# An add that read its constant from a PSUM bank now reads it from SBUF, in a new instruction order (attention and mixture kernel, one core)

## The chip, the cores and the metric

The kernel runs on one core of a Trainium2 chip. The metric is the device time of one execution in microseconds (us). Five engines work side by side, each through its own queue in order: TensorE (PE in the rows; its weight loads are PEld), VectorE (DVE), ScalarE (ACT), GpSimd (POOL) and SyncE (SP), which here only issues DMAs. They meet through semaphores: an instruction may wait for a count that another engine's instruction raises when it ends. PE writes only into PSUM, which has 8 banks per partition; DVE and ACT read PSUM and SBUF; POOL reads SBUF.

## The reference, cut to what matters

For 8 batches and 8 heads (sequence 576, head dimension 64) attention keeps only scores close to the row's maximum:

```python
scores = scale * np.matmul(q, k.transpose(0, 1, 3, 2))
thresh = np.max(scores, axis=-1, keepdims=True) - tau
scores = np.where(scores >= thresh, scores, -1000000000.0)
attn = np.exp(scores - max); attn = attn / (sum + 1e-09)
x = attn @ v
```

Then a mixture runs per batch on x (576 x 512): `theta = x @ w_theta`, `zr = x * cos(theta)`, `zi = x * sin(theta)`, `u = x + w_tok_r @ zr + w_tok_i @ zi`, and the output is `u + relu(u @ w_ch)`. All of it is float32; most products are done as three passes over a high and a low part of each operand.

## The kernel before, in words

Heads are worked in 32 pairs n, each in 5 units i: units 0 to 3 take 128 queries of both heads of the pair, unit 4 the last 64 queries of both in one tile. Per unit:

- PE writes the scores (L797, 12 matmuls for two heads, 6 for unit 4) into PSUM: two banks per head. From pair 5 on there is one place for it, banks 0 to 3 (unit 4: banks 0 and 1, or 2 and 3); the first five pairs take turns between banks 0 to 3 and 4 to 7.
- DVE evicts each head's scores to SBUF (tile `sc`) and reduces the row minimum of the negated, scaled scores into `nm` on the way (L817: one instruction and a short accumulator read).
- DVE adds the span `cut` to these minima (L827, the **add**). It is 160 small instructions in the kernel: 128 for two heads (128x2), 32 for one tile (128x1).
- ACT takes the result as a bias: L838 masks, L845 takes the exponential and its row sum.
- DVE transposes in blocks of 32 (L857, L859) into `a`.

Per pair PE then multiplies by v (L874, two parts of 72 matmuls, also into banks 0 to 3), ACT copies the result out (L887, L890), and the row sums are inverted (L900, L901) and spread by DMA. Every fourth pair a batch is full and its mixture is fed into the PE queue between the scores of the next batch: L982 (channel products), L1125 (transposes), L1170 (token products); these use banks 2 to 7. POOL and DVE make the low parts (L527), POOL multiplies (L1100, L928). In the first 170 us the weights are split as well (lines 577 to 669).

The constant that L827 adds lies in PSUM, in two columns of bank 0 that no matmul writes:

```python
cuts = psum[:, 0, 508:510]
nc.vector.tensor_scalar(out=cuts, in0=cut.broadcast_to([P, 2]), scalar1=1.0, scalar2=None, op0=ALU.mult)
```

What stands when in each engine's queue is set by a table, not by a rule that runs: `Plan` collects the operations, and `run()` issues them by the numbers in `ORDER`, with the buffer of each tile taken from `PLACES`. Semaphore waits are put in by the framework underneath, from the tiles and banks that instructions touch; `Plan` itself knows nothing of the read of bank 0 by L827 (its argument `over` names `nm` and `small` alone).

Of the kernel before, what the change touches and what calls it, by code (L numbers as in the profile page):

```python
# [14 lines left out]
ALU = mybir.AluOpType  # L15
# [49 lines left out]
        "0101201210002121201201210210212012120101201021021012010201212010211021"  # L65
    ),
    "xl": (
        "002130211031201232130120301230123012301231023012320130123102301230123012310230123"
    ),
    "xh": (  # L70
        "20012031202031202031130123102301210310201302130123120301230213012302130123120301231203012302130123"
    ),
    "rb": (
        "010101011001010110010001101110010101101000111000"
    ),
    "bank": (
        "73733223675445237632450444004430004447000044604004437643567456754736747656475457465657740000002000000300"
        "00007000000757464657322346275746467475546767546600000040000006000000400000036745765476372635746535676447"
        "65456767000000400000050000007000000745675467574754676574764777754567454600000040000007000000600000066765"
        "74657472675764574566774574564747000000400000040000007000000765545767444657436754564557674556754600000040"  # L80
        "00000500000050000006745645764523426557546564764576777645000000600000060000007000024523475673237434235742"
        "63753467324546"
    ),
    "z": (
        "1012010212001200120012001200120012001200120"
    ),
    "q": (
        "02131023102130213021302130213021302130213021302130213210312"
    ),
    "k": (  # L90
        "02310210321032103210321032103210321032103210321032103210321"
# [5 lines left out]
        "01235976841870231576241035179203102516470235891053145264073154210352406174213056802345126015340241320132"  # L97
        "31402301401526304125064782102312034512436012405212031456710358203461025410231426301521042357682051342610"
        "43501425012340531260351741230451620537112056032415768395410326705401451024321560"
    ),  # L100
    "nm": (
        "01232031032301012012031201202130012100213120102123100120201230102310123012010012301021023102130210213101"
        "20312013021311201010213101201231310210012301230301231010"
# [8 lines left out]
        "01234560132460513426150243610254"  # L112
# [8 lines left out]
        "0123012301231023012310230123012301231023013213020123012301231023"  # L121
    ),
    "zl4": (
        "0123102301231023012301320123012301230123012301230123013201230123"
# [8 lines left out]
        "011000010101010110101101010"  # L133
# [281 lines left out]
def tile_attn_moe(  # L415
# [43 lines left out]
    nc.vector.memset(half_pi, 0.5 * math.pi)  # L459
    magic = small[:, 4 : 5]  # L460
    nc.vector.memset(magic, MAGIC)
    cuts = psum[:, 0, 508:510]
    wt_h = const.tile([P, NK, S], F32R, name="wt_h")
    wt_l = const.tile([P, NK, S], F32R, name="wt_l")
    wm_dram = dram.tile([2, NM, P, 2, NM, P], F32, name="wm_dram")
# [881 lines left out]
```

## Time and profile before

| | |
|---|---|
| time, median of 3 runs | 937.41 us (931.9, 937.41, 938.98) |
| profiled execution, its own time | 931.98 us |
| its span, first to last instruction | 930.2 us |
| PE busy | 858.5 us (92%) |
| ACT busy | 692.4 us (74%) |
| DVE busy | 684.3 us (74%) |
| POOL busy | 340.7 us (37%) |

PE is busy nearly all the time, so the question at any place is what PE waits for there. A matmul that has no wait follows the one before at a distance shorter than its own duration, so busy PE is not PE at its peak.

### The profile page before, as it was taken

To read this page: it belongs to the slowest core of one execution; us is meant where nothing else is said; L and a number is where in the kernel's file an instruction comes from. 1 tells how busy PE (TensorE), PEld (TensorE's weight loads), DVE (VectorE), ACT (ScalarE), POOL (GpSimd) and SP (SyncE) were. 2 spreads that over 40 slices of the span, in tenths; PEclk is the share of its full clock that TensorE was granted. 3 is DMA by queue.
4 is the path that set the end of the run, shared out by engine and by line. 5 is a ranking of instruction groups with operands and counts; after the bars stand their busy time and mean duration, and the time that the engine had idled before them with its cause. 6 is when DMAs were issued, how large, how long until landed. Compare 5 with 4: busy or idle time off the path is not lost.

```text
span 930.2 us, 33724 instructions
## 1 busy us (share of the span) xinstructions
PE 858.5 (92%) x14526; PEld 764.7 (82%) x14526; DVE 684.3 (74%) x1545; ACT 692.4 (74%) x1390; POOL 340.7 (37%) x444
## 2 busy tenths in 40 slices
PE   6677899899999999999999999999999999999998
PEld 3554688788987889988888889988799889988898
DVE  7979878976677885778777876787966768777443
ACT  6986798766876689866898659956898569976550
POOL 1248555533432234523432344232344233431211
PEclk9899999999999999999999999999999999999999
DMA  7546542445323451246432333235633354213502
GB/s 275 177 142 213 172 148 93 143 151 189 145 93 106 160 178 68 80 138 216 164 106 93 114 120 138 105 133 166 190 108 101 98 179 167 89 66 136 188 2 74
DMA packets 45286, 126.13 MB, mean 136 GB/s; under 512 B 5456, under 2 KB 14544, under 8 KB 41040
## 3 DMA queue, kind: packets, MB, share of 16 engines
q1 hardware_dynamic: 44992, 123.97, 39.6%
q8 instruction: 114, 1.87, 0.8%
q14 instruction: 36, 0.29, 0.1%
q10 hardware_dynamic: 144, 0.00, 0.0%
HBM read 110.17 MB, written 13.78 MB: 133 GB/s over the span
## 4 chain that ended last, share of the span: by engine, by line
PE 64%; DVE 21%; ACT 6%; issue 5%; POOL 2%; DMA 1%; SPq 0%; DVEq 0%; ACTq 0%; POOLq 0%
PE banks_ps__66 L1170 18%; PE banks_ps__66 L874 15%; PE banks_ps__66 L797 14%; PE banks_ps__66 L982 12%; DVE sc L817 10%; DVE a L857 5%; PE banks_ps__66 L1125 3%; DVE nm L827 1%; ACT sc L838 1%; DMA v<-in_vp_dram 1%; ACT sc L845 1%; POOL xl L527 1%; PE banks_ps__66 L663 1%; DVE xl L527 1%; DVE xh L603 1%
## 5 line engine op out<-in xcount | busy, mean ns | idle before, releaser
L838 ACT ACTIVATE sc<-sc,nm 128x576 f32<-128x576 f32 x288 | 216.7, 771 | 104.5 <-DVE nm L827 104.2
L817 DVE TENSOR_SCALAR_CACHE_REDUCE sc<-banks_ps__66,small 128x576 f32<-128x576 f32 x288 | 224.4, 808 | 41.4 <-PE banks_ps__66 L797 35.4
L845 ACT ACTIVATE sc<-sc,small 128x576 f32<-128x576 f32 x288 | 222.6, 774 | 4.8
L857 DVE STREAM_TRANSPOSE a<-sc 128x576 f32<-128x576 f32 x256 | 188.7, 759 | 31.0 <-PE banks_ps__66 L874 23.7
L797 PE MATMUL banks_ps__66<-k,q 64*128 64x288 f32 (+1 forms) x1638 | 175.7, 324 | 36.3 <-DVE nm L827 22.5
L797 PEld LDWEIGHTS banks_ps__66<-k,q 64*128 64x128 f32 (+1 forms) x1638 | 132.0, 187 | 70.7 <-DVE nm L827 37.0
L874 PE MATMUL banks_ps__66<-a,v 32*64 32x144 f32 x9216 | 168.7, 289 | 15.2 <-issue 6.0
L874 PEld LDWEIGHTS banks_ps__66<-a,v 32*64 32x64 f32 x9216 | 148.9, 132 | 30.5 <-issue 14.5
L982 PE MATMUL banks_ps__66<-xh,wm 128*128 128x288 f32 x1024 | 169.6, 302 | 3.5 <-issue 1.5
L1170 PE MATMUL banks_ps__66<-wt_h,zh 128*128 128x288 f32 x576 | 160.6, 305 | 1.1 <-ACT zh L1131 1.1
L1170 PE MATMUL banks_ps__66<-wt_l,zh 128*128 128x288 f32 x576 | 158.7, 300 | 0.0
L982 PEld LDWEIGHTS banks_ps__66<-xh,wm 128*128 128x128 f32 x1024 | 143.5, 188 | 14.9 <-issue 10.7
L527 POOL TENSOR_TENSOR xl<-xT,xh 128x288 fp32r<-128x288 f32 x78 | 67.1, 881 | 178.3 <-ACT xh L941 82.1
L1100 POOL TENSOR_TENSOR z<-z,xT 128x288 f32<-128x288 f32 x112 | 88.4, 824 | 95.4 <-ACT z L1081 95.4
L1170 PEld LDWEIGHTS banks_ps__66<-wt_h,zh 128*128 128x128 f32 x576 | 107.9, 189 | 5.6 <-issue 3.1
L1170 PEld LDWEIGHTS banks_ps__66<-wt_l,zh 128*128 128x128 f32 x576 | 108.2, 188 | 2.1 <-issue 2.0
L1170 PE MATMUL banks_ps__66<-wt_h,zl 128*128 128x288 f32 x576 | 96.2, 301 | 0.0
L982 PE MATMUL banks_ps__66<-xl,wm 128*128 128x288 f32 x512 | 94.8, 302 | 1.0 <-POOL xl L527 0.3
L1150 DVE TENSOR_TENSOR zl<-banks_ps__66,zh 128x512 fp32r<-128x512 f32 (+1 forms) x96 | 51.5, 547 | 47.7 <-ACT zh L1131 47.6
L1170 PEld LDWEIGHTS banks_ps__66<-wt_h,zl 128*128 128x128 f32 x576 | 81.1, 188 | 2.7 <-issue 2.5
L527 POOL TENSOR_TENSOR q<-rawq,q 128x320 fp32r<-128x320 f32 x54 | 49.1, 917 | 86.8 <-DVE q L732 64.8
L982 PEld LDWEIGHTS banks_ps__66<-xl,wm 128*128 128x128 f32 x512 | 75.4, 188 | 6.0 <-issue 2.9
(81 smaller groups left out, 921.6 us busy)
## 6 DMA issues: line engine op xcount, KB each, us to landing
v<-in_vp_dram SPq DMA_DIRECT2D x32, 1152.0 KB
wm<-wm_dram SPq DMA_DIRECT2D x64, 512.0 KB
rb<-sums_dram SPq DMA_DIRECT2D x64, 144.0 KB
out_dram<-xT SPq DMA_DIRECT2D x31, 288.0 KB
rawq<-in_qT_dram SPq DMA_DIRECT2D x27, 320.0 KB
rawk<-in_kT_dram SPq DMA_DIRECT2D x27, 288.0 KB
z<-in_w_tok_dram SPq DMA_DIRECT2D x9, 576.0 KB
wm_dram<-rb SPq DMA_DIRECT2D x16, 256.0 KB
```

The costliest lines, as they stand in the source:

```text
L527: eng.tensor_tensor(out=out()[:, c0:c1], in0=in0()[:, c0:c1], in1=in1()[:, c0:c1], op=ALU.subtract)
L797: nc.tensor.matmul(ps()[:, 2 * j + h, :HS], q[a]()[r, i * P : (i + 1) * P], k[c]()[r, h * HS : (h + 1) * HS], start=(x == 0), stop=(x == l ...
L817: lambda j=j, sc=sc: nc.vector.tensor_scalar(out=sc().rearrange("p (a b) -> p a b", a=2), in0=ps()[:, 2 * j : 2 * j + 2, :HS], scalar1=gat ...
L838: lambda j=j, sc=sc: nc.scalar.activation(out=sc(), in_=sc(), func=AF.Prelu, bias=nm()[:, 2 + j : 3 + j], scale=-1.0, alpha=STEEP),
L845: lambda j=j, sc=sc, total=total: nc.scalar.activation(out=keys(sc()), in_=keys(sc()), func=AF.Exp, bias=back, accum_out=pr.rows()[:, tota ...
L857: nc.vector.transpose(out=a()[:, :, j, 32 * i : 32 * i + 32], in_=src.rearrange("p (c q) -> p c q", q=32))
L874: nc.tensor.matmul(ps()[64 * h : 64 * h + 64, b, :w], v()[r, c, h, :], a()[r, c, h, :], start=(c == 0), stop=(c == 17))
L982: nc.tensor.matmul(ps[h]()[:, :HS], wm()[:, a, c, :], parts[c][bb]()[:, h * HS : (h + 1) * HS], start=first and n == 0, stop=final and n = ...
L1100: eng.tensor_tensor(out=zi, in0=zi, in1=x[m]()[:, c0:c1], op=ALU.mult)
L1125: nc.tensor.transpose(out=tp()[:, i * P : (i + 1) * P], in_=z()[:, c : c + P], identity=ident)
L1150: lambda zh=zh, zl=zl, tv=tv: nc.vector.tensor_tensor(out=zl(), in0=tv(), in1=zh().bitcast(F32), op=ALU.subtract),
L1170: nc.tensor.matmul(ps()[:, :HS], zz[c][lo]()[:, zz[c][2]], w[:, c, hs], start=(q + n == 0), stop=(q + n == len(work) - 1),)
```

## The change

Two edits. First, the add takes its constant as a per-partition scalar from SBUF (`cut`, a column of `small`), so it is a tensor_scalar and no longer a tensor_tensor; the copy in PSUM and the instruction that wrote it (L545) are gone. Second, the tables `ORDER` and `PLACES` are new throughout: all instructions but the one are the same, in another order on every engine, and in other buffers. Line numbers fall by up to 3 (L817 is L814, L827 is L824, L874 is L871, and so on).

```diff
@@ PLACES (most entries differ)
     "nm": (
-        "01232031032301012012031201202130012100213120102123100120201230102310123010012010301021023102130210213101"
+        "01232012031201210210231013002130012021013120120123101021201230102310231212010012301021023102130210213101"
...
@@ ORDER (134 lines for 135)
-    "202 1 -3 5 -205 206 1 1 -7 14 1 29 -28 29 -28 -7 -210 1 1 209 2 -210 1 242 -12 1 1 -231 6 197 1 42 -1 3 2 -1 "
+    "203 -1 -202 200 5 2 -6 -200 1 213 -9 11 -1 -8 10 -7 8 -10 36 -242 1 242 -241 242 1 -13 -229 6 225 15 -1 -15 18 "
...
@@ tile_attn_moe
-    cuts = psum[:, 0, 508:510]
...
@@ factors()
-        nc.vector.tensor_scalar(out=cuts, in0=cut.broadcast_to([P, 2]), scalar1=1.0, scalar2=None, op0=ALU.mult)
...
@@ unit()
         dve(
             0.15,
-            lambda: nc.vector.tensor_tensor(out=nm()[:, 2 : 2 + w], in0=nm()[:, :w], in1=cuts[:, :w], op=ALU.add),
+            lambda: nc.vector.tensor_scalar(out=nm()[:, 2 : 2 + w], in0=nm()[:, :w], scalar1=cut, scalar2=None, op0=ALU.add),
             t0 + A("add", n), over, ((nm, 2),), small=True,
         )
```

**PE, scores of one unit of a late pair.** Two rows of before, with the semaphores each waits for: the first matmul of the twelve has the one wait on DVE.

```order
L797 MATMUL banks_ps__66<-k,q 128x288 [waits DVE_49]
L797 MATMUL banks_ps__66<-k,q 128x288 x11
L905 MATMUL banks_ps__66<-ident,rows 9x128 [waits DVE_49,Activation_49]
L982 MATMUL banks_ps__66<-xl,wm 128x288 x4
L982 MATMUL banks_ps__66<-xh,wm 128x288 x4
```

And the same place (the 24th L905, now L902) with the change:

```order
L794 MATMUL banks_ps__66<-k,q 128x288 [waits DVE_49] x2
L794 MATMUL banks_ps__66<-k,q 128x288 x10
L902 MATMUL banks_ps__66<-ident,rows 9x128 [waits DVE_49,Activation_49]
L979 MATMUL banks_ps__66<-xh,wm 128x288 x4
L979 MATMUL banks_ps__66<-xl,wm 128x288 x4
```

The one wait has become two, one on each of the first two matmuls (they write the first bank of head 0 and of head 1). In the built program of before, 87 first matmuls of scores and 26 of values wait for a count that an add raises; with the change none does, and the waits of scores on L817 (now L814) rise from 56 to 155. In the other direction 27 adds waited for PE before, and none does now.

**DVE, about 727 us into the span of before.** The add on `nm_11485` belongs to the last unit whose scores are evicted ahead of a multiplication by v.

```order
L817 TENSOR_SCALAR sc_11484,nm_11485<-banks_ps__66,small_76 128x576 [waits DVE_49,PE_49,Activation_49]
L817 TENSOR_SCALAR sc_11498,nm_11485<-banks_ps__66,small_76 128x576
L857 STREAM_TRANSPOSE a_11315<-sc_11395 128x18x32 [waits Activation_49]
L900 TENSOR_SCALAR rows_11201<-rows_11201 128x9 [waits Activation_49]
L901 RECIPROCAL rows_11201<-rows_11201 128x9 [waits DVE_49]
L859 STREAM_TRANSPOSE a_11315<-sc_11412 128x36x16
L857 STREAM_TRANSPOSE a_11315<-sc_11075 128x18x32
L857 STREAM_TRANSPOSE a_11315<-sc_11392 128x18x32
L1182 TENSOR_TENSOR xT_10323<-banks_ps__66,xT_10323 128x288 [waits DMAHW1_49,PE_49,Pool_49]
L1182 TENSOR_TENSOR xT_10323<-banks_ps__66,xT_10323 128x288
L943 CAST xh_11554<-xT_10323 128x576 [waits DVE_49]
L827 TENSOR_TENSOR nm_11485<-nm_11485,banks_ps__66 128x2
```

With the change (the last unit ahead of the multiplication is `nm_11531` there):

```order
L814 TENSOR_SCALAR sc_11464,nm_11465<-banks_ps__66,small_76 128x576 [waits DVE_49,PE_49]
L814 TENSOR_SCALAR sc_11467,nm_11465<-banks_ps__66,small_76 128x576
L856 STREAM_TRANSPOSE a_11296<-sc_11432 128x36x16 [waits Activation_49]
L897 TENSOR_SCALAR rows_11185<-rows_11185 128x9 [waits Activation_49]
L898 RECIPROCAL rows_11185<-rows_11185 128x9 [waits DVE_49]
L824 TENSOR_SCALAR nm_11465<-nm_11465,small_76 128x2
L854 STREAM_TRANSPOSE a_11296<-sc_11394 128x18x32
L814 TENSOR_SCALAR sc_11530,nm_11531<-banks_ps__66,small_76 128x576 [waits PE_49]
L814 TENSOR_SCALAR sc_11539,nm_11531<-banks_ps__66,small_76 128x576 [waits PE_49]
L824 TENSOR_SCALAR nm_11531<-nm_11531,small_76 128x2 [waits DVE_49]
L854 STREAM_TRANSPOSE a_11296<-sc_11369 128x18x32
L854 STREAM_TRANSPOSE a_11296<-sc_11366 128x18x32
```

Before, the last add stood behind four transposes, the two evictions of the mixture (L1182) and a cast (L943); now it stands right behind its two evictions.

## Rows read from the trace of the kernel before

**Rows 1.** The page, part 1: busy time, share of the span, instructions by engine.

```profile
PE 858.5 (92%) x14526; PEld 764.7 (82%) x14526; DVE 684.3 (74%) x1545; ACT 692.4 (74%) x1390; POOL 340.7 (37%) x444
```

**Rows 2.** Busy time by stretch: PE, PEld, DVE, ACT, POOL; granted clock; DMA share; GB/s.

```profile
0.00:186.00 186.00, 147.97 (x2459) 118.32 (x2460) 156.48 (x345) 149.56 (x303) 91.40 (x138) 0.97 0.52 170
186.00:860.00 674.00, 645.80 (x11357) 583.44 (x11364) 498.74 (x1147) 518.34 (x1042) 239.42 (x294) 1.00 0.39 131
860.00:930.20 70.20, 64.77 (x728) 62.98 (x712) 29.04 (x55) 24.52 (x46) 9.89 (x12) 1.00 0.27 88
```

**Rows 3.** Waits of PE, whole span: us in total, times, longest.

```profile
PE banks_ps__66 L797 <- DVE nm L827: 22.5, 35, 2.8
PE banks_ps__66 L797 <- DVE sc L817: 6.4, 6, 1.8
...
PE banks_ps__66 L874 <- DVE nm L827: 4.2, 9, 1.5
```

**Rows 4.** Waits of PE from 186 us to the end.

```profile
PE banks_ps__66 L797 <- DVE nm L827: 13.3, 26, 1.3
PE banks_ps__66 L874 <- DVE nm L827: 3.9, 8, 1.5
```

**Rows 5.** Line 827: durations (min/median/max ns), then what it waited for (us, times).

```profile
L827 DVE TENSOR_TENSOR nm<-nm,banks_ps__66 x160: 97/155/158, 8.4 to 855.1; 128x2 f32<-128x2 f32 x128, 128x1 f32<-128x1 f32 x32
...
  PE banks_ps__66 L874: 29.0, 14
  PE banks_ps__66 L797: 6.3, 8
```

**Rows 6.** Timeline at 200 us: start, duration, engine, line; in brackets idle before and releaser.

```profile
200.53 0.08 DVE L817 DVE_READ_ACCUMULATOR sc<-banks_ps__66,small 128x1 f32 x1
200.64 0.16 DVE L827 TENSOR_TENSOR nm<-nm,banks_ps__66 128x2 f32<-128x2 f32 x1
...
200.85 1.07 PE L797 MATMUL banks_ps__66<-k,q 64*128 64x288 f32 x12 [0.61 <-DVE nm L827]
```

**Rows 7.** Timeline, 506 to 509 us, DVE and PE.

```profile
506.37 0.16 DVE L827 TENSOR_TENSOR nm<-nm,banks_ps__66 128x2 f32<-128x2 f32 x1 [0.70 <-PE banks_ps__66 L797]
...
507.84 0.08 DVE L817 DVE_READ_ACCUMULATOR sc<-banks_ps__66,small 128x1 f32 x1
...
508.54 0.12 DVE L827 TENSOR_TENSOR nm<-nm,banks_ps__66 128x1 f32<-128x1 f32 x1
...
508.71 1.07 PE L797 MATMUL banks_ps__66<-k,q 64*128 64x288 f32 x12 [1.06 <-DVE nm L827]
```

**Rows 8.** Timeline, 727 to 733 us, DVE and PE.

```profile
727.88 0.08 DVE L817 DVE_READ_ACCUMULATOR sc<-banks_ps__66,small 128x1 f32 x1
...
732.30 0.46 DVE L943 CAST xh<-xT 128x576 fp32r<-128x576 f32 x1
732.68 0.15 DVE L827 TENSOR_TENSOR nm<-nm,banks_ps__66 128x2 f32<-128x2 f32 x1
...
732.89 2.51 PE L874 MATMUL banks_ps__66<-a,v 32*64 32x144 f32 x144 [1.53 <-DVE nm L827]
```

**Rows 9.** Groups of lines, shapes apart: busy us, mean ns of one, idle before.

```profile
L827 DVE TENSOR_TENSOR nm<-nm,banks_ps__66 128x2 f32<-128x2 f32 x128 | 18.2, 147 | 33.4 <-PE banks_ps__66 L874 29.0 <-PE banks_ps__66 L797 2.5
...
L900 DVE TENSOR_SCALAR rows<-rows 128x9 f32<-128x9 f32 x32 | 7.0, 220 | 0.0
```

**Rows 10.** Line 900: min/median/max ns.

```profile
L900 DVE TENSOR_SCALAR rows<-rows x32: 128/166/692, 25.5 to 857.8; 128x9 f32<-128x9 f32 x32
```

**Rows 11.** Timeline at 519 us, POOL and DVE.

```profile
519.06 0.81 POOL L527 TENSOR_TENSOR xl<-xT,xh 128x288 fp32r<-128x288 f32 x1 [2.69 <-DVE xh L943]
519.27 0.63 DVE L900 TENSOR_SCALAR rows<-rows 128x9 f32<-128x9 f32 x1
```

**Rows 12.** Timeline at 6 us, DVE.

```profile
5.81 0.16 DVE L545 TENSOR_SCALAR banks_ps__66<-small 128x2 f32<-128x2 f32 x1 [1.45 <-PE banks_ps__66 L797]
...
6.77 0.82 DVE L817 TENSOR_SCALAR_CACHE_REDUCE sc<-banks_ps__66,small 128x576 f32<-128x576 f32 x1 [0.74 <-PE banks_ps__66 L797]
```

**Rows 13.** Timeline at 919 us, PE: twelve matmuls with no wait among them.

```profile
919.43 1.75 PE L982 MATMUL banks_ps__66<-xh,wm 128*128 128x288 f32 x12
```

More of the change, by code (lines that the diff above doesn't have):

```diff
@@ L64 @@
     "wm": (
-        "0101201210002121201201210210212012120101201021021012010201212010211021"
+        "0101201210002121201012210212010210012010212012102110210102220101201201"
     ),
     "xl": (
-        "002130211031201232130120301230123012301231023012320130123102301230123012310230123"
+        "003120311030201232130120301230123012301231023012320130123102301231023012301230123"
     ),
     "xh": (
-        "20012031202031202031130123102301210310201302130123120301230213012302130123120301231203012302130123"
+        "20012031202013201312021032120301203010021302130123012301231023012301230123102301231203012302130123"
@@ L72 @@
     ),
     "rb": (
-        "010101011001010110010001101110010101101000111000"
+        "011001010101010110010001100010100110011101011000"
     ),
     "bank": (
-        "73733223675445237632450444004430004447000044604004437643567456754736747656475457465657740000002000000300"
-        "00007000000757464657322346275746467475546767546600000040000006000000400000036745765476372635746535676447"
-        "65456767000000400000050000007000000745675467574754676574764777754567454600000040000007000000600000066765"
@@ L80 @@
-        "74657472675764574566774574564747000000400000040000007000000765545767444657436754564557674556754600000040"
-        "00000500000050000006745645764523426557546564764576777645000000600000060000007000024523475673237434235742"
-        "63753467324546"
+        "73733232323232576757640404004430004447000044604044065764754675675432645676447757467657544400003000000300"
+        "00007000000575466475323465775467656477745654757600000060000007000000700000077465476543742356476657466554"
+        "76456567000000300000060000007000000746576475654464756657465777744756475400000030000004000000700000055774"
@@ L83 @@
+        "56745532644754764577744664575646000000500000050000006000000675475674765764237567465747657456754600000050"
+        "00000400000070000006476575647523752446577754664657575364000000700000030000004000026423645734242667547325"
+        "63472357326437"
     ),
     "z": (
-        "1012010212001200120012001200120012001200120"
+        "0120121020101200120012001200120012001200120"
     ),
     "q": (
-        "02131023102130213021302130213021302130213021302130213210312"
+        "02103021302130213021302130213021302130213021302130213210312"
@@ L89 @@
     ),
     "k": (
-        "02310210321032103210321032103210321032103210321032103210321"
+        "02313021320132013201320132013201320132013201320132013201320"
     ),
@@ L96 @@
     "sc": (
-        "01235976841870231576241035179203102516470235891053145264073154210352406174213056802345126015340241320132"
-        "31402301401526304125064782102312034512436012405212031456710358203461025410231426301521042357682051342610"
-        "43501425012340531260351741230451620537112056032415768395410326705401451024321560"
+        "01233876845920305176180243109763140583261045795823045264073154210232416074213056802345126013040231420131"
+        "30432130403516204305126785021320134502436012435021342156702358210462135401230426312504210357680253142601"
+        "32501435012340531260351740231450632417210356032415768597021436257412450124301563"
     ),
     "nm": (
-        "01232031032301012012031201202130012100213120102123100120201230102310123012010012301021023102130210213101"
-        "20312013021311201010213101201231310210012301230301231010"
+        "01232012031201210210231013002130012021013120120123101021201230102310231212010012301021023102130210213101"
+        "20312013021310210101203121201032110210021320132001231010"
     ),
@@ L111 @@
     "xT": (
-        "01234560132460513426150243610254"
+        "01234560321406531420356142031564"
     ),
@@ L120 @@
     "zh4": (
-        "0123012301231023012310230123012301231023013213020123012301231023"
+        "0123012301231023012310230123012301231023013213020123012301230123"
     ),
     "zl4": (
-        "0123102301231023012301320123012301230123012301230123013201230123"
+        "0123102301231023012301320123012301230123012301230123012301230123"
     ),
@@ L132 @@
     "rawq": (
-        "011000010101010110101101010"
+        "011011010101010100110111101"
     ),
```

255 rows, old and new, of the table ORDER are left out of this document.

## The prediction, made before the changed kernel ran

> **What bounds the kernel now.** I read the page's busy times first, then busy time by stretch, then the waits of PE, then the timeline around the longest of these waits. PE is busy for 858.5 us of 930.2 and no other engine for more than 74% [rows 1], so the end moves with PE's idle time: 930.2 - 858.5 = 71.7 us. By stretch [rows 2], 38.0 us of it lie in the first 186 us (186.0 - 148.0), where DVE is busy for 84% and the weights are split; 28.2 us lie between 186 and 860 us, and 5.4 us in the last 70 us, when no scores are left. The waits of PE name one thing above all: scores and values that wait for the add, 22.5 + 4.2 = 26.7 us in 44 places [rows 3], of which 13.3 + 3.9 = 17.2 us come after 186 us [rows 4]. That is the odd entry: PE needs nothing that the add computes. What it needs is the bank, and the bank is free when L817 has evicted it. The add stands between them only because it reads its constant from bank 0. The same tie runs the other way: DVE stood idle for 29.0 + 6.3 = 35.3 us ahead of the add until PE was done with bank 0 [rows 5].
>
> **The tie goes.** The reader should see three forms of it. At 200.85 us the second eviction's accumulator read ends at 0.53 + 0.08 = 200.61, the add runs from 200.64 to 200.80, and PE starts at 200.85 after 0.61 us idle [rows 6]. Freed by the eviction itself, PE could start 0.05 us after 200.61 (the hand-over after the add, 200.85 - 200.80), so 0.19 of the 0.61 us go. At 508.71 us the last eviction ended at 507.92, but a transpose stands between it and the add, and PE idles 1.06 us [rows 7]: by the same rule, 508.71 - 507.97 = 0.74 us go. The DVE queue itself was late there, because the add of the unit before had waited 0.70 us for PE [rows 7]; that part is not counted. At 732.89 us the last eviction ended at 727.96 and the add came 4.7 us later, behind transposes, two evictions and a cast; all of 1.53 us goes [rows 8]. I did this subtraction, capped at the idle time, for all 44 places: 16 are of the first form (add right behind the eviction) and lose 3.2 of 7.5 us; 28 are of the other two and lose 18.1 of 19.3 us. Sum 21.3 us, 6.6 of it before 186 us and 14.7 behind. Bounds: from 44 x 0.16 = 7 us (only the add's own length, as in rows 6) to all 26.7 us.
>
> Not all of it reaches the end. In the first stretch PE is fed by DVE at 84% and ACT at 80% [rows 2], so what PE gains it meets again as a wait for a split weight or an eviction; I keep half, 3.3 us. Behind 186 us DVE and ACT stand at 74% and 77% of the middle stretch [rows 2], and late next is the eviction: twelve matmuls between two score groups cover (1.75 - 0.30) / 11 x 12 = 1.58 us [rows 13], about as much as two evictions take. I keep three quarters, 11.0 us. **Term 1: -14.3 us.**
>
> **The add's new form.** The trace has no tensor_scalar on two elements that reads SBUF behind a busy GpSimd. The nearest rows are L900, a tensor_scalar between SBUF operands on nine elements: median 166, mean 220 ns, least 128, most 692 [rows 9, 10]. The old add took 147 ns on the mean and never more than 158 [rows 5, 9]. What lies between L900's median and mean is a wait now and then: at 519.27 us it took 0.63 us and ended at 519.90, just behind a GpSimd operation that ran from 519.06 to 519.87 [rows 11]. So I price the add at 160 + 54 = 214 ns, 67 ns more than before, 160 x 0.067 = 10.7 us of DVE. Below: 128 ns, a gain of 3 us of DVE. Above: GpSimd is busy 37% of the span [rows 1] with operations of 0.81 us [rows 11], so an add would wait 0.37 x 0.41 = 0.15 us, 24 us in all. DVE has 26% to spare, and PE no longer waits for the add itself, only for evictions queued behind it and, through ACT, for transposes. I let a fifth through. **Term 2: +2.1 us** (0 to 24).
>
> The Trainium skill has a rule that speaks against this edit: "SBUF — State Buffer", section "Who interferes with whom", says that a tensor_scalar between SBUF operands can take the port pair that VectorE shares with GpSimd, and that whoever comes second then stands still for the other's whole instruction; the old add, with one operand in PSUM, would not have met it. Row 519.27 agrees with that; the median of L900 says that most instances escape. Taken at its word for every add, the rule would give the upper price of 24 us and, if all of it reached PE, 931.98 - 14.3 + 24 - 2 = 939.7 us.
>
> **Removed.** L545 (0.16 us) and its wait of 1.45 us for PE stand at the start [rows 12], but the first eviction behind it waits for PE anyway, another 0.74 us. Worth nothing; its cover is PE's first scores, which come no earlier.
>
> **The new order.** Every queue is reshuffled: DMAs on SP, POOL's products, the buffers. The amount of work is the same, and so are the stages: the same groups follow each other, and between score groups from pair 5 on there stand 2.06 us of other matmuls on the mean, before it was 2.11 (counted in the order, at 0.132 us each from rows 13). At the place of rows 8 the add has moved up behind its evictions, and the values follow the last scores after 27 other matmuls in place of 36. What a better order could still win is PE's idle time without the adds, 71.7 - 26.7 = 45 us, most of it in the first stretch; what a worse one could lose has no bound in the trace. I take a small gain, since the placing of adds and evictions looks tighter where I read it. **Term 3: -2 us** (+10 to -10).
>
> **Sum.** 931.98 - 14.3 + 2.1 - 2.0 = 917.8 us against the profiled execution's own time. That execution equals the fastest of the three runs shown (931.9); their median, 937.41, is 5.4 us above. A median of the changed kernel lies between 917.8 and 923.2; I take the middle: **920 us**.
>
> **Rivals.** The same half step of 2.7 us is added to each.
>
> *More is freed (0.17).* If all 26.7 us go and a part of DVE's 35.3 us of waiting comes back as earlier evictions, as rows 7 suggest (say 5 us): 931.98 - 26.7 - 5 + 2.7 = 903 us. For it: the add blocked both queues. Against it: PE, ACT and DVE would all have to run closer to full.
>
> *The wait is only renamed (0.23).* The eviction ends just before the add, so PE waits for L814 in place of L824 and saves the add's length alone, 7 us, less 2.1 us: 931.98 - 7 + 2.1 + 2.7 = 929.8 us, range 925 to 934. For it: the form of rows 6 and PE's 6.4 us of waits for L817 already there [rows 3]. Against it: 28 of the 44 places.
>
> *GpSimd's hold slows it (0.06).* Each add, and through it each eviction behind it on DVE, stands behind a GpSimd operation: 24 us as above, all of it reaching PE at the scores, while only 7 us are freed: 931.98 + 24 - 7 + 2.7 = 952 us. It cancels terms 1 and 3 once 16 us of such holds reach PE; with only 7 us freed, the kernel is slower by 1% (946.8 us) from 19 us on. Against it: L900's 54 ns. This is the mechanism of the Trainium skill's rule named above.
>
> *The change doesn't do what it says (0.04).* The waits could stay under another instruction's name, with the new order neutral: 932 to 938 us. The order speaks against it: no add waits for PE, and scores wait for evictions in two steps.
>
> **Range and chances.** The forecast (0.50) has its own range of 914 to 925 us. To reach 8 in 10 I add most of the first rival and the lower part of the second: 905 to 931 us. A measurement of this kernel can tell about 1% (9.4 us) from no change. Faster by more than that means below 928.0 us: the forecast, the first rival and a third of the second, 0.50 + 0.17 + 0.07 = 0.74. Within 1%: the rest of the second and the last, 0.16 + 0.04 = 0.20. Slower: 0.06.
>
> **What would show it.** In the changed profile: no wait of PE or DVE names L824 together with PE; PE's waits for L814 rise from 6.4 us but stay under 15; L824 lasts about 0.2 us on the mean with a few instances over 0.5 us that end with a GpSimd operation; PE's idle time falls from 71.7 to about 57 us, two thirds of the fall after 186 us. Term 1 is wrong if PE's idle falls by less than 8 us with those waits gone; term 2 if evictions end later behind long adds; term 3 if PE's idle changes mainly at waits that never named the add.

## The result, and the profile after

The changed kernel took 907.88 us in the median of 4 runs (906.83 to 912.85), the kernel before 936.62 us on the same chip. The ratio is 0.9708, with a 95% interval of 0.9663 to 0.9753: faster by 2.9%. The forecast was 920 us with a range of 905 to 931. The time lies in the range, but 6 us below the forecast's own range of 914 to 925, between it and the rival "more is freed" (903 us). Measured again later, the changed kernel took 905.13 us, ratio 0.9646 [0.9606, 0.9686].

The profiled execution is the slowest of the four (912.85 us, span 911.0). The page, part 1, of the changed kernel, which answers to [rows 1]:

```profile
PE 864.1 (95%) x14526; PEld 772.4 (85%) x14526; DVE 704.0 (77%) x1544; ACT 692.6 (76%) x1390; POOL 344.5 (38%) x444
```

PE's idle time is 911.0 - 864.1 = 46.9 us, where it was 71.7. The span fell by 19.2 us and the idle time by 24.8, because busy PE rose by 5.6 us for the same matmuls. The stretches, answering to [rows 2] (the middle one now ends at 840 us):

```profile
0.00:186.00 186.00, 155.87 (x2565) 123.13 (x2573) 162.28 (x350) 149.57 (x304) 95.56 (x140) 0.95 0.52 173
186.00:840.00 654.00, 642.76 (x11244) 585.37 (x11231) 512.74 (x1140) 518.04 (x1040) 236.93 (x290) 0.99 0.39 134
840.00:911.00 71.00, 65.44 (x741) 63.87 (x740) 29.01 (x56) 24.97 (x46) 12.03 (x14) 1.00 0.26 87
```

Idle PE is 30.1, 11.2 and 5.6 us, where it was 38.0, 28.2 and 5.4: 17.0 of the 24.8 us, two thirds, came from the middle stretch. The rise of busy PE is a matter of the start. The first 90 us of the changed kernel:

```profile
0.00:90.00 90.00, 67.93 (x1080) 46.14 (x1081) 73.28 (x175) 69.76 (x141) 38.40 (x70) 0.91 0.58 197
```

And of the kernel before:

```profile
0.00:90.00 90.00, 61.63 (x1075) 41.97 (x1075) 75.11 (x181) 70.11 (x142) 38.27 (x72) 0.96 0.60 202
```

Nearly the same number of matmuls took 6.3 us more of PE at a mean granted clock of 0.91 in place of 0.96. The gain of this profiled execution (19.2 us) is smaller than that of the medians (28.7).

The waits of PE for scores, over the whole span, answering to [rows 3]:

```profile
PE banks_ps__66 L794 <- DVE sc L814: 5.5, 11, 1.3
```

The 26.7 us of waits for the add are gone from scores and values, and waits for the eviction did not take their place. From the answer on line 824, answering to [rows 5]:

```profile
L824 DVE TENSOR_SCALAR nm<-nm,small x160: 168/224/942, 10.5 to 835.4; 128x2 f32<-128x2 f32 x128, 128x1 f32<-128x1 f32 x32
its engine sat idle before it (us, times) until:
who waited for it (us, times):
  ACT sc L835: 79.5, 50
```

The second line has nothing under it: DVE never sits idle ahead of the add. Of PE's matmuls only one at L902 (0.2 us) still waits for it. How this looks in time shows at 711 us. DVE and PE in the changed kernel (start, duration):

```profile
710.68 0.81 DVE L814 TENSOR_SCALAR_CACHE_REDUCE sc<-banks_ps__66,small 128x576 f32<-128x576 f32 x1
711.42 0.08 DVE L814 DVE_READ_ACCUMULATOR sc<-banks_ps__66,small 128x1 f32 x1
711.42 0.77 DVE L856 STREAM_TRANSPOSE a<-sc 128x576 f32<-128x576 f32 x1
...
711.66 0.29 PE L1167 MATMUL banks_ps__66<-wt_l,zh 128*128 128x288 f32 x1
711.89 1.06 PE L794 MATMUL banks_ps__66<-k,q 64*128 64x288 f32 x12
...
712.91 0.17 DVE L824 TENSOR_SCALAR nm<-nm,small 128x2 f32<-128x2 f32 x1
```

The second eviction of the unit ends at 711.50, PE starts the next scores at 711.89 with no wait on its row, and the add of the evicted unit comes only at 712.91, behind a transpose and the inversion of row sums. In [rows 8], PE stood still for an add that came late in this way.

The add's new form became longer than priced. The groups of the changed kernel by shape (busy us, mean ns), answering to [rows 9]:

```profile
L824 DVE TENSOR_SCALAR nm<-nm,small 128x2 f32<-128x2 f32 x128 | 37.6, 299 | 2.3
L897 DVE TENSOR_SCALAR rows<-rows 128x9 f32<-128x9 f32 x32 | 7.5, 234 | 0.6 <-ACT sc L842 0.6
L824 DVE TENSOR_SCALAR nm<-nm,small 128x1 f32<-128x1 f32 x32 | 6.4, 200 | 0.6
```

### The profile page after: what moved, and what is told of

Its sections match the earlier page's. It is cut to its first block, busy times and chain, and to the rows that moved or that the text cites. A ratio compares the mean times of both kernels' runs of the same rounds, so it can differ in the third digit from the quotient of the medians.

```text
span 911.0 us, 33697 instructions
## 1 busy us (share of the span) xinstructions
PE 864.1 (95%) x14526; PEld 772.4 (85%) x14526; DVE 704.0 (77%) x1544; ACT 692.6 (76%) x1390; POOL 344.5 (38%) x444
## 4 chain that ended last, share of the span: by engine, by line
PE 71%; DVE 15%; ACT 6%; issue 3%; POOL 2%; DMA 2%; SPq 0%; DVEq 0%; ACTq 0%; POOLq 0%
PE banks_ps__66 L1167 23%; PE banks_ps__66 L979 16%; PE banks_ps__66 L871 16%; PE banks_ps__66 L794 12%; DVE sc L814 6%; DVE a L854 4%; PE banks_ps__66 L1122 3%; ACT sc L835 1%; ACT sc L842 1%; POOL xl L525 1%; DVE nm L824 1%; DMA v<-in_vp_dram 1%; DVE xh L600 1%; DVE z L1047 1%; DVE zl L1147 1%
## 5 line engine op out<-in xcount | busy, mean ns | idle before, releaser
L814 DVE TENSOR_SCALAR_CACHE_REDUCE sc<-banks_ps__66,small 128x576 f32<-128x576 f32 x288 | 223.1, 805 | 20.6 <-PE banks_ps__66 L794 18.9
L794 PE MATMUL banks_ps__66<-k,q 64*128 64x288 f32 (+1 forms) x1638 | 181.3, 329 | 13.2 <-DVE sc L814 5.5
L871 PE MATMUL banks_ps__66<-a,v 32*64 32x144 f32 x9216 | 169.8, 289 | 12.0 <-issue 6.9
L794 PEld LDWEIGHTS banks_ps__66<-k,q 64*128 64x128 f32 (+1 forms) x1638 | 136.4, 190 | 45.5 <-DVE sc L814 17.0
L979 PE MATMUL banks_ps__66<-xh,wm 128*128 128x288 f32 x1024 | 172.6, 304 | 1.2 <-issue 0.6
L871 PEld LDWEIGHTS banks_ps__66<-a,v 32*64 32x64 f32 x9216 | 149.1, 132 | 27.5 <-issue 17.2
L979 PEld LDWEIGHTS banks_ps__66<-xh,wm 128*128 128x128 f32 x1024 | 145.4, 190 | 12.8 <-issue 8.9
L525 POOL TENSOR_TENSOR k<-rawk,k 128x288 fp32r<-128x288 f32 x54 | 45.7, 852 | 77.3 <-DVE k L755 30.5
```

The source lines that it names most:

```text
L525: eng.tensor_tensor(out=out()[:, c0:c1], in0=in0()[:, c0:c1], in1=in1()[:, c0:c1], op=ALU.subtract)
L794: nc.tensor.matmul(ps()[:, 2 * j + h, :HS], q[a]()[r, i * P : (i + 1) * P], k[c]()[r, h * HS : (h + 1) * HS], start=(x == 0), stop=(x == l ...
L814: lambda j=j, sc=sc: nc.vector.tensor_scalar(out=sc().rearrange("p (a b) -> p a b", a=2), in0=ps()[:, 2 * j : 2 * j + 2, :HS], scalar1=gat ...
L871: nc.tensor.matmul(ps()[64 * h : 64 * h + 64, b, :w], v()[r, c, h, :], a()[r, c, h, :], start=(c == 0), stop=(c == 17))
L979: nc.tensor.matmul(ps[h]()[:, :HS], wm()[:, a, c, :], parts[c][bb]()[:, h * HS : (h + 1) * HS], start=first and n == 0, stop=final and n = ...
```

## The experiments

Theory T: the tie through bank 0 was the cost, and its removal is the gain. Rival O: the new order is the gain. A second question is what the add's new form costs (term 2). Each ratio is against runs of the kernel before on the same chip. The median of the kernel before was 936.6 to 939.1 us from one set of runs to the next, so kernels of different sets are compared by their ratios, and 0.001 of a ratio is 0.94 us.

**The SBUF add alone, in the order of before** (e1_add_only). Edit on the kernel before:

```diff
-    cuts = psum[:, 0, 508:510]
-        nc.vector.tensor_scalar(out=cuts, in0=cut.broadcast_to([P, 2]), scalar1=1.0, scalar2=None, op0=ALU.mult)
-            lambda: nc.vector.tensor_tensor(out=nm()[:, 2 : 2 + w], in0=nm()[:, :w], in1=cuts[:, :w], op=ALU.add),
+            lambda: nc.vector.tensor_scalar(out=nm()[:, 2 : 2 + w], in0=nm()[:, :w], scalar1=cut, scalar2=None, op0=ALU.add),
```

> The order and buffers of before, the add reads its constant from SBUF. Theory T (the tie through bank 0 is the gain): 0.980 to 0.986 of before, 918 to 924 us, no wait of PE names the add, PE's idle time down by about 14 us from 71.7. Rival O (the new order is the gain): 0.995 to 1.005, 932 to 941 us, with PE's waits renamed to the evictions.

Measured: 911.56 us (909.26 to 915.65), ratio 0.9728 [0.969, 0.9767]. Nearly the whole gain comes without the new order, and it is larger than theory T had it (918 to 924 us): PE's idle time is 913.8 - 865.0 = 48.8 us, 22.9 less than before, where about 14 was expected. Its waits of PE for evictions:

```profile
PE banks_ps__66 L795 <- DVE sc L815: 9.6, 14, 2.1
PE banks_ps__66 L661 <- DVE sc L815: 1.1, 1, 1.1
PE banks_ps__66 L872 <- DVE sc L815: 0.3, 1, 0.3
```

No wait names the add, and 34.4 us of waits for add and eviction together became 11.0.

**The new order alone, with the constant in bank 0** (e2_order_only): the changed kernel, with the three lines above turned back.

> The order and buffers of the change, the add reads its constant from PSUM bank 0 as before. Theory T: 0.986 to 1.000 of before, 924 to 937 us, with 20 us or more of PE waits that name the add. Rival O: 0.968 to 0.978, 907 to 916 us, the tie being covered by the new order.

Measured: 949.03 us (943.03 to 956.56), ratio 1.0127 [1.0066, 1.0188]: slower by 1.3%. Rival O falls, and the time is above theory T's range too. The tie costs more in this order than in the old one, 949.0 - 907.9 = 41 us against 26. Not all of that is waiting: in the profiled executions (spans 954.8 and 911.0 us) 33.5 us of the difference are idle PE (80.4 against 46.9) and 10.3 busy PE (874.4 against 864.1), at a mean granted clock of 0.975 in place of 0.985. Waits of PE:

```profile
PE banks_ps__66 L796 <- DVE nm L826: 24.6, 25, 4.0
PE banks_ps__66 L873 <- DVE nm L826: 7.4, 9, 2.2
```

**The constant in bank 1** (e8_bank_one), the kernel before with one digit changed:

```diff
-    cuts = psum[:, 0, 508:510]
+    cuts = psum[:, 1, 508:510]
```

> The kernel before with its constant in bank 1 (same columns) in place of bank 0, order and form of the add unchanged. Each unit's first two matmuls write banks 0 and 2, the third is the first on bank 1, so what waited for the add at the first matmul now waits two matmuls later, 2 x 0.132 = 0.26 us. Theory T (the wait for the bank of the constant is the cost): of the 44 waits of before, 26.8 us, the first 0.264 us of each are covered, 10.7 us in sum; the wait for the eviction then counts on the first matmul, so 4 to 10 us come free: 928 to 934 us against 938, ratio 0.990 to 0.996, and PE's waits for L827 fall to 14 to 20 us. Rival E (only evictions count, or reads of PSUM by themselves are slow): no change, 0.998 to 1.002.

Measured: 931.12 us (929.09 to 933.35), ratio 0.9939 [0.9922, 0.9955]. That is theory T's range: the add still reads PSUM, and only the matmul that has to wait for it has moved by two. The trace shows the move, here at 531 us:

```profile
530.40 0.40 PE L797 MATMUL banks_ps__66<-k,q 64*128 64x288 f32 x2
531.55 0.93 PE L797 MATMUL banks_ps__66<-k,q 64*128 64x288 f32 x10 [0.76 <-DVE nm L827]
```

Its line 827:

```profile
  PE banks_ps__66 L874: 29.4, 14
  PE banks_ps__66 L797: 8.4, 11
...
  PEld banks_ps__66 L797: 14.0, 30
  PE banks_ps__66 L797: 6.6, 11
  PEld banks_ps__66 L874: 6.8, 12
...
  PE banks_ps__66 L874: 1.7, 3
```

PE waits for the add for 6.6 + 1.7 = 8.3 us, less than the 14 to 20 I expected, and more for evictions (11.9 us in all). The first two rows are DVE's own idle time ahead of the add: 37.8 us, no less than the 35.3 of [rows 5]. PE's waits for both fell by 14.2 us, and the time by only 5.8.

**The add left out** in the changed kernel (e3_no_add) and in the old order (e7_no_add_old_order). Both use the bare minima as bias, so the span is missing from the result:

```diff
-            lambda: nc.vector.tensor_scalar(out=nm()[:, 2 : 2 + w], in0=nm()[:, :w], scalar1=cut, scalar2=None, op0=ALU.add),
+            lambda: None,
-                    out=sc(), in_=sc(), func=AF.Prelu, bias=nm()[:, 2 + j : 3 + j], scale=-1.0, alpha=STEEP
+                    out=sc(), in_=sc(), func=AF.Prelu, bias=nm()[:, j : j + 1], scale=-1.0, alpha=STEEP
```

> The change with the add left out: the span is not added to the maxima, ACT takes the bare minima as its bias. It takes 44 us of DVE work away (37.6 + 6.4 by the profile of the change). If DVE has slack and PE does not wait behind the adds: 902 to 908 us, at most 5 us below the change. Rival, the holds by GpSimd reach PE: 890 to 899 us.

> The kernel before in its own order with the add left out (bare minima as bias). It bounds what the tie and the add were worth together in that order. If what the tie frees is the add's wait alone: the SBUF add in this order gave 911.6, and leaving it out took 7.7 us in the new order, so 904 us (899 to 908). If the new order is better by itself once the tie is gone, this run is slower than the changed kernel without the add (900.2) by 3 to 5 us; if the order is worth nothing, within 2 us of it.

Measured: e3 900.21 us, ratio 0.9612 [0.9569, 0.9654]; e7 903.0 us, ratio 0.9616 [0.9582, 0.965]. e3 lies between its two ranges. By the ratios, the add's price in the changed kernel is 0.9708 - 0.9612, or 9 us (3 us against its later 0.9646), and in the old order 0.9728 - 0.9616, or 10 us. Each of these differences is uncertain by some 5 us. Busy DVE fell from 704.0 to 673.0 us in e3:

```profile
PE 860.9 (95%) x14526; PEld 771.8 (85%) x14526; DVE 673.0 (74%) x1384; ACT 692.3 (77%) x1390; POOL 345.1 (38%) x444
```

So 31.0 us of DVE cost about 3 to 9 us of time, 10 to 29%.

**The add twice** (e5_add_twice), the changed kernel:

```diff
+            lambda: [
                 nc.vector.tensor_scalar(out=nm()[:, 2 : 2 + w], in0=nm()[:, :w], scalar1=cut, scalar2=None, op0=ALU.add) for _ in range(2)
+            ],
```

> The changed kernel with every add issued twice in a row (same operands, same result). Dose for the add's price. Theory P (the add's time on DVE reaches PE in part): leaving the add out took 31.0 us of busy DVE away and 7.7 us of time, a quarter; a second add puts about 128 x 0.30 + 32 x 0.20 = 45 us on DVE (704 to about 748 us), so 11 us of time: 919 us (914 to 926). Rival H (only that ACT waits for an add at all counts, its length does not): within 3 us of the changed kernel, 905 to 911. Rival S (DVE is so close to late that all of it comes through): above 935 us.

Measured: 930.99 us (930.36 to 933.12), ratio 0.9928 [0.9904, 0.9951]. Its page, part 1:

```profile
PE 873.6 (94%) x14526; PEld 775.8 (83%) x14526; DVE 746.1 (80%) x1704; ACT 694.1 (75%) x1390; POOL 344.4 (37%) x444
```

And its waits of PE at the scores:

```profile
PE banks_ps__66 L794 <- DVE sc L814: 13.5, 23, 1.6
```

The second dose cost 21 to 26 us by the ratios (0.9928 against 0.9708 and 0.9646) for 42.1 us of DVE (746.1 - 704.0), 49 to 63% of it, where the first dose cost 10 to 29%. Theory P, which took the price as proportional, falls; so does S in its size. Evictions queued behind adds now come late: 13.5 us in 23 places in place of 5.5 in 11. The price of small DVE work rises with the dose. How much of that is DVE being late stays open: of the 18.1 us between the two spans (929.1 and 911.0) only 8.6 are idle PE, and 9.5 are busy PE for the same matmuls, at a mean granted clock of 0.980 in place of 0.985.

**The form of the add.** Two tensors from SBUF (e6_two_tensors), the changed kernel with its constant in a tile `cuts` of two columns in SBUF:

```diff
+    cuts = const.tile([P, 2], F32, name="cuts")
+        nc.vector.tensor_scalar(out=cuts, in0=cut.broadcast_to([P, 2]), scalar1=1.0, scalar2=None, op0=ALU.mult)
-            lambda: nc.vector.tensor_scalar(out=nm()[:, 2 : 2 + w], in0=nm()[:, :w], scalar1=cut, scalar2=None, op0=ALU.add),
+            lambda: nc.vector.tensor_tensor(out=nm()[:, 2 : 2 + w], in0=nm()[:, :w], in1=cuts[:, :w], op=ALU.add),
```

> The changed kernel, its order kept, with the add as a tensor_tensor again, its constant in two columns of a tile in SBUF. It tells whether the tensor_scalar form is what GpSimd holds up. If it is the form (two operands from SBUF are free of it): L824 mean about 150 ns and none above 0.2 us, DVE busy 704 to about 684 us, time 903 us (900 to 907). If an add with two operands in SBUF is held too: mean 200 to 300 ns with some over 0.5 us that end with a GpSimd operation, and 905 to 911 us. In both cases no wait of PE names L824.

Measured: 906.86 us (905.89 to 908.9), ratio 0.9662 [0.963, 0.9694]; not to be told from the change. This form is held up too. Two waits of matmuls in the first 44 us (L873, 1.8 us) still name the add, which was not expected; the add no longer touches a bank. Its line 826:

```profile
L826 DVE TENSOR_TENSOR nm<-nm,cuts x160: 99/160/1940, 10.4 to 831.6; 128x2 f32<-128x2 f32 x128, 128x1 f32<-128x1 f32 x32
```

And the longest instance, with GpSimd beside it:

```profile
513.76 0.82 POOL L526 TENSOR_TENSOR k<-rawk,k 128x288 fp32r<-128x288 f32 x1
...
514.18 1.94 DVE L826 TENSOR_TENSOR nm<-nm,cuts 128x2 f32<-128x2 f32 x1
...
514.54 1.57 POOL L927 TENSOR_TENSOR xT<-xT,rb 128x288 f32<-128x288 f32 x2
```

The add starts while one GpSimd operation runs and ends at 516.12, 0.01 us behind the second of the two that follow it (514.54 + 1.57 = 516.11).

Then one-element adds (e4_two_singles, and once more beside the changed kernel, e4_again and after_again):

```diff
+            lambda: [
+                nc.vector.tensor_scalar(out=nm()[:, 2 + j : 3 + j], in0=nm()[:, j : j + 1], scalar1=cut, scalar2=None, op0=ALU.add)
+                for j in range(w)
+            ],
```

> The change with the add of two heads as two instructions on 128x1, which by the profile of the change last 0.17 to 0.22 us each and are never held up. No instance over 0.25 us. If the holds (25 of 128 adds, up to 0.94 us) cost time: 3 to 6 us below the change. Rival, DVE slack covers them: within 2 us of the change, or 1 to 3 us above it for 160 more short instructions.

> The changed kernel with the add of two heads as two adds of one element each, once more and in more rounds. Theory G (the holds by GpSimd are most of the add's price; one-element adds escape them): 2 to 4 us under the changed kernel, as the 905.5 against 907.9 us of the earlier runs. Rival N (an additional 128 instructions use up what the holds gave): within 1 us of it.

> The changed kernel once more, beside the version with two one-element adds: 907 us (905 to 910).

Measured: 905.54 us, ratio 0.9677 [0.9629, 0.9725]; then 902.96 us, ratio 0.9628 [0.9586, 0.967], beside 905.13 us, 0.9646 [0.9606, 0.9686], for the changed kernel. Twice it is lower, by 2.9 us (0.9677 against 0.9708) and by 1.7 us (0.9628 against 0.9646), and twice the intervals overlap, so it stays open whether it is the better version. The line of e4_again:

```profile
L825 DVE TENSOR_SCALAR nm<-nm,small x288: 153/205/216, 10.1 to 826.4; 128x1 f32<-128x1 f32 x144
```

Not one of 288 is held, but there are 288 instructions of about 203 ns where there were 160.

**One-element adds in the old order** (e9_old_order_singles): the first experiment with this add.

> The kernel before in its own order, with the SBUF add as one-element adds. If the new order is worth nothing without the tie: the same as the changed kernel's version with one-element adds, within 2 us. If the order is worth the 3.7 us that lay between the two orders with the SBUF add of two elements (911.6 and 907.9 us): 908 to 910 us.

Measured: 907.31 us (903.71 to 911.03), ratio 0.9673 [0.9629, 0.9718]. With it there are three pairs that differ in the order alone, all without the tie. Old and new order have ratios of 0.9728 and 0.9708 (later 0.9646) with the two-element add, 0.9616 and 0.9612 without an add, 0.9673 and 0.9628 (earlier 0.9677) with one-element adds. Of these pairs only 0.9673 and 0.9628 were measured side by side. The new order is thus better by 1.9 to 7.7 us, by 0.4 us, and by 4.2 us or not at all. The intervals overlap in all of them but the widest (0.9728 against 0.9646), which comes from two sets of runs. A small gain is likely, but its size is not settled.

**The kernel before once more**, for a second profile (before_again).

> The kernel before once more, for a second profile. The stretch up to the 64th eviction of scores took 181.28 us in the first profile at a granted clock of 0.88 to 1.00 in steps of 23 us, and 181.96 us with the SBUF add at 0.83 to 0.98. If the clock of the first 90 us is chance and hides a gain there: this profile is slower in that stretch (184 to 190 us) at a lower clock, and its rest, from the 64th eviction to the last, is 673 us again within 2. If the gain before 181 us is zero: 181 to 182 us again.

Measured: 940.77 us, span 939.0. The stretch up to the 64th score eviction took 184.71 us (181.28 in the first profile), within the range of the first reading, but not for its reason: the mean granted clock there is 0.97 in both profiles. And the rest up to the last eviction took 677.97, 5.0 us more than the 672.99 of the first. So the difference is no matter of the start alone, and a single profile places a stretch of this length no better than to about 5 us.

## Why the prediction was right in direction and short in size

**The tie goes: right, and the mechanism is shown.** With the add alone the waits and 25.9 us of time went (937.5 to 911.56); with the order alone neither did; moving the constant by one bank moved the wait and 0.6% of the time. The rival "only renamed" would have had the waits come back at L814; they stand at 5.5 us, and stood at 6.4 [rows 3]. The Trainium skill, "PSUM — Partial Sum Buffer", section "PSUM bank collisions raise a hardware error", says to guard PSUM with semaphores by bank and quadrant of 32 partitions (in its simple version by bank), not by address. The 26.7 us of waits [rows 3] for two columns that no matmul writes are such a guard's price here, and in the run with bank 1 the wait at the scores moved to the first matmul on that bank.

**Term 1, the failed step: "Not all of it reaches the end".** The working kept half of the first stretch and three quarters of the rest, -14.3 us. The stretch from the start of the 64th score eviction to that of the 288th is the same work in the first experiment as before, for the order is the same. Before:

```profile
181.28:854.27 672.99, 644.79 (x11332) 582.38 (x11332) 497.50 (x1144) 515.22 (x1036) 240.77 (x296) 1.00 0.39 131
```

With the SBUF add:

```profile
181.96:837.57 655.61, 643.26 (x11330) 584.79 (x11330) 511.73 (x1144) 515.27 (x1037) 241.07 (x296) 1.00 0.39 134
```

It is shorter by 17.4 us, and by 22.4 against the second profile of before. The waits for the add in it were 13.3 + 3.9 = 17.2 us [rows 4]. So as far as these profiles can tell, all of them reached the end, although DVE did 14.2 us more; I had put down 11.0. The argument that evictions would be late next was wrong in size: PE waited for evictions for 2.2 us in this stretch of the first experiment, and for 0.7 us in 2 places behind 186 us in the changed kernel:

```profile
PE banks_ps__66 L794 <- DVE sc L814: 0.7, 2, 0.4
```

In the stretch ahead of it, half was to be met again as waits. What the rows show there is another thing. Before, and with the SBUF add:

```profile
0.00:181.28 181.28, 143.25 (x2420) 113.92 (x2421) 152.06 (x336) 148.54 (x301) 88.48 (x134) 0.97 0.52 171
0.00:181.96 181.96, 151.30 (x2424) 120.11 (x2425) 154.24 (x334) 148.12 (x300) 86.93 (x134) 0.92 0.51 170
```

PE's idle time fell by 7.4 us (38.0 to 30.7), but nearly the same matmuls took 8.0 us more at a granted clock of 0.92 in place of 0.97. The other profiles point the same way: this stretch has 143 to 145 us of busy PE in the three with the tie and the old order (clock 0.97), and 146 to 155 in the ten without the tie (clock 0.92 to 0.97); the new order with the tie has 150 as well. So most of what the start gained in this profile went into busy PE, and not into other waits.

The subtraction itself was made on a row that shows too little. PE's row of waits counts idle time of the matmul queue. The weight loads' queue waits too, and a part of that lies beside matmuls that still run. I had not read that row. In the kernel before:

```profile
PEld banks_ps__66 L797 <- DVE nm L827: 37.0, 55, 3.0
...
PEld banks_ps__66 L797 <- DVE sc L817: 12.3, 23, 2.2
PEld banks_ps__66 L874 <- DVE nm L827: 9.0, 20, 1.8
```

And in the changed kernel:

```profile
PEld banks_ps__66 L794 <- DVE sc L814: 17.0, 44, 1.8
...
PEld banks_ps__66 L871 <- DVE sc L814: 1.8, 9, 0.4
PEld banks_ps__66 L794 <- DVE nm L824: 1.6, 10, 0.2
...
PEld banks_ps__66 L871 <- DVE nm L824: 0.5, 3, 0.2
```

The tie held weight loads for 46.0 us in 75 places, not 26.7 in 44. Summed over all lines, waits for the add and the eviction stand like this in the kernels with the order of before:

| kernel | PE waits, us | weight loads wait, us | median, us |
|---|---|---|---|
| before | 34.4 | 59.5 | 936.6 to 939.1 |
| constant in bank 1 | 20.2 | 46.0 | 931.1 |
| SBUF add | 11.0 | 27.6 | 911.6 |
| SBUF add, one element each | 10.1 | 25.9 | 907.3 |
| no add | 7.7 | 19.7 | 903.0 |

From before to the SBUF add, PE's waits fell by 23.4 us, the weight loads' by 31.9, the time by 25.9, between the two. The second row of the table seems to fit neither: 14.2 and 13.5 us of waits less brought 5.8. The stretch from the 64th to the 288th score eviction tells where a part of it went, with the constant in bank 1 and in the second profile of the kernel before:

```profile
180.93:850.83 669.90, 651.32 (x11332) 587.76 (x11332) 496.03 (x1145) 515.08 (x1037) 240.19 (x296) 1.00 0.38 132
184.71:862.68 677.97, 646.85 (x11332) 584.32 (x11332) 496.77 (x1143) 515.51 (x1036) 240.31 (x296) 1.00 0.39 130
```

PE's idle time is 18.6 us, 9.6 and 12.5 us less than in the two profiles of before, but its busy time is 6.5 and 4.5 us more at the same granted clock. At 530.40 us the first two matmuls ran until 530.80 and the third came at 531.55: of the 1.15 us between their starts only 0.76 stands as a wait, and the rest as busy PE. So a wait that begins behind matmuls still running is worth more than PE's idle time says. DVE's own waiting for PE ahead of the add (37.8 us) was left too, which the prediction set aside ("that part is not counted"). What this direction costs by itself is not shown: no run took away one direction alone and left the other untouched.

**Term 2, mis-sized, though its mechanism was right.** The price was 214 ns an add, 67 ns more than before; in the changed kernel it is 299 ns with two elements and 200 ns with one, and busy DVE rose by 19.7 us in place of 10.7. Two things were missed. The least and the median are 168 and 224 ns where the nearest row had 128 and 166 [rows 10]: L900 takes its constant from the instruction, the add reads it from SBUF, which may be the reason; no run isolates it. And GpSimd's holds were more: 26 of the 128 two-element adds took 0.31 to 0.94 us. One of them in the changed kernel, at 159 us, with GpSimd beside it:

```profile
158.94 1.31 POOL L1097 TENSOR_TENSOR z<-z,xT 128x288 f32<-128x288 f32 x1
159.51 0.77 DVE L824 TENSOR_SCALAR nm<-nm,small 128x2 f32<-128x2 f32 x1
```

The add ends at 160.28, 0.03 us behind GpSimd. The share that reaches the end agrees with the forecast at this dose within the noise (a fifth; 10 to 29% for the whole add) and would have been far too low at twice the dose (half or more). The rule in the Trainium skill, "SBUF — State Buffer", section "Who interferes with whom", that the prediction weighed, agrees with these holds and with the two-tensor form's, but the 24 us that it would give if it struck every add were not reached: the whole add costs about 3 to 9.

**Term 3 and the removed L545.** The order was worth 0 to 8 us in the three pairs, against the 2 us put down; nothing there is clear enough of noise to correct the term. What the prediction did not see is that a gain can hold only without the tie; with it the new order is 1.3% slower than the old one. L545 was worth nothing, as said: the first eviction of scores starts at 7.12 us now and started at 6.77 [rows 12].

**What was to show it.** PE's idle time was to fall to about 57 us with two thirds of the fall after 186 us: it fell to 46.9, two thirds after 186 us. PE's waits for L814 at the scores were to rise from 6.4 us and fell to 5.5, which again says that evictions were not late. No pair of L824 with scores or values was left on PE, and L824 has instances of over 0.5 us that end with a GpSimd operation. L824's mean was to be about 0.2 us and is 0.275 (37.6 + 6.4 us over 160).

**The sum again**, in medians. The tie with the add's new price is -25.9 us where -14.3 + 2.1 = -12.2 stood, and the order -3.7 (911.56 to 907.88) where -2.0 stood; together that is 15.4 us lower. The half step to the median was 2.7 us too small: every run of the kernel before taken since then took 932.92 us or more, so the profiled execution's 931.98 us was a fast one and the whole 5.4 us belonged there. 917.8 + 5.4 - 15.4 = 907.8 us, and 907.88 were measured. The sum closes because both steps are differences of these same medians; it is no further evidence. What is shown is the sign and rough size of the tie's term: its discount was the error. That the time lies inside the range is owed to the first rival, for whose sake the range went down to 905 us: all 26.7 us freed and 5 more from DVE's side made 903, nearer than the forecast's 920.

## What to carry to other kernels

A small vector instruction that reads a constant from a PSUM bank makes PE wait for it and makes it wait for PE: look for waits of PE on something whose result PE does not use, and move the constant before tuning an order around the tie. Size such a tie by the waits of the weight loads as well as PE's, compare busy PE at equal work and its granted clock too, and do not discount the sum for the next engine unless a row shows that engine late. The price of added vector work is not proportional: the first 31 us cost about 3 to 9 us here, the next 42 cost 21 to 26.

## What the runs showed of the hardware that was not expected

No tensor_scalar on one element from SBUF shows a hold by GpSimd: the longest of 288 took 0.23 us. With two elements it took up to 0.94 us. A tensor_tensor with both operands in SBUF is held in either shape; this is one of the one-element adds of the two-tensor form, with GpSimd beside it:

```profile
751.86 1.74 POOL L526 TENSOR_TENSOR q<-rawq,q 128x320 fp32r<-128x320 f32 x2 [6.23 <-DVE q L731]
...
752.87 0.75 DVE L826 TENSOR_TENSOR nm<-nm,cuts 128x1 f32<-128x1 f32 x1
```

It ends at 753.62, 0.02 us behind GpSimd. The add with its constant in SBUF takes about 60 ns longer than the nearest instruction with its constant in itself (medians 224 and 165 ns, L824 and L897). The two differ in shape as well, so that the place of the constant is the reason is not shown.
